# Two FNet and gated layers on one core: the second layer's downs of blocks two to four in seven products over six tile pairs

## The chip, the cores and the metric

The kernel runs on one core of a Trainium2 chip. TensorE (PE, with PEld for its weight loads), VectorE (DVE), ScalarE (ACT), GpSimd (POOL) and SyncE (SP, which here only issues DMAs) each run their own list of instructions in order and meet through semaphores. The metric is the device time of one execution in microseconds (us).

## The reference

The input x has 2048 rows of 640 numbers; the function is two equal layers, each an FNet mixing and a gated unit of width 1728 (the three weights are drawn eight times as large as the sizes 0.05 suggest).

```python
def _A_ref(x, dft_seq_re, dft_seq_im, dft_hid_re, dft_hid_im):
    a = jnp.einsum("bsd,ed->bse", x, dft_hid_re)
    b = jnp.einsum("bsd,ed->bse", x, dft_hid_im)
    return jnp.einsum("ts,bse->bte", dft_seq_re, a) - jnp.einsum("ts,bse->bte", dft_seq_im, b)

def _B_ref(x, w_gate, w_up, w_down):
    g = jnp.einsum("bsd,df->bsf", x, w_gate)
    u = jnp.einsum("bsd,df->bsf", x, w_up)
    return jnp.einsum("bsf,fd->bsd", _sigmoid(g) * u, w_down)

x = A_x
for _ in range(2):
    x = x + _A_ref(_layernorm(x, axis=-1), ...)
    x = x + _B_ref(_layernorm(x, axis=-1), B_w_gate, B_w_up, B_w_down)
return x
```

## The kernel before

**Numbers.** A float32 number is held as a high and a low float16 part; a product is three passes (high by high, high by low, low by high) summed in PSUM in float32. ACT makes a high part by a copy, DVE the low part by a subtraction.

**Tiles.** The 2048 rows are four blocks (NB) of 512 rows, a block four tiles (TB) of 128 rows. The gated width of 1728 is 13 full tiles of 128 (NF) and a tail of 64, tile 13. In layer 2, blocks two to four are b = 1, 2, 3 in the code.

**Gate and up of a block** (`seven`, from L1517). For each of the 13 tiles j, the products of the tile's gate and up weights with the block's turned rows are made by seven products of combined operands instead of eight; two tiles share one step. The rows, combined and turned (features on partitions), stand in `XW[place(b)]`, and two such places alternate. The gate's and up's results come out as 128x512 numbers `hv`; `up_parts` (L1508) splits them into a high and a low part (`ht`, L1513 on ACT and L1514 on DVE).

**Down of a block** (`down`, from L1593). For each of its four row tiles the 41 products (13 tiles by three passes, two for the tail) run into two PSUM banks, one for each half of the 640 columns: 328 matmuls of 128x320 in a block, and two adds onto x for each row tile (L1618). In layer 2 each finished row tile is then stored to the output (`store_x`, L442 and L447).

**Next block's rows.** While block b-1 is in its downs, the rows of block b are made in two pairs of row tiles, i = 0 and 1: `pair_stats`, `pair_scale`, `pair_apply` (L603), `pair_combine` (L610 to L613), `pair_parts` (L621, L622, four pieces) and `pair_transpose` (L628), which issues two DMA transposes on SP, one for the high and one for the low parts. PE needs all four before the first product of block b.

**Weights.** They are split once in layer 1 and kept in DRAM (`kept_w`, `kept_s`). `load_s` (L1362) brings the gate, combined and up weights of tile j back: three loads on SP (L1363, L1365, and L1367 or L1369).

**Structure tests.** The program tests that the DFT matrices have the structure that it uses. In layer 2, `load_hidden_rows` (L1724) loads rows of the hidden matrix from POOL's DMA queue, and DVE compares them (L1728, and L1687 to L1690 for the sequence matrix); `test_all` (L1761 on) gathers the results.

**What sets the order.** All work around the products is put at a time on a line of steps, `at(u, function, ...)`, where u counts steps from the start of the program and `block[b]` is the first of block b: a block has 14 for gate and up (one for each tile) and eight for its downs. Whatever falls to a step is written into the program there, and each engine runs what it gets in that order. Homes in SBUF are given by `Slots` and `find_homes`, which run once ahead without homes to learn who lives when; the areas for turned rows and for the down weights stand outside of them, in front of FIX.

The lines that set the rows' and first loads' times:

```python
u = block[b] - 8 + 1.2 * i
...
    at(u + 0.2 + 0.2 * n, pair_parts, b, i, n)
at(u + 1.1, pair_transpose, b, i, not first and b == last)
...
at(u - 2 - 0.5 * (j % 2) if j > 3 else block[b] - ((5.9, 3, 2, 1.5) if first and b == 1 else (8, 7.9, 4.5, 3.5))[j], load_s, j, not first and b == last)
```

## Time and profile before

| | |
|---|---|
| time, median of 3 runs | 1135.06 us (1134.55 to 1135.15) |
| span of the profiled execution | 1133.3 us |
| the profiled execution's own time | not listed apart; the median is 1.8 us above its span, taken as what lies around it |
| PE busy | 1117.1 us (99%) |
| DVE, ACT, POOL busy | 67%, 48%, 31% |
| four downs of layer 2 | 44.72 us each |
| gate and up of layer 2's third block | 79.7 us |

A group's row gives line, engine, operation, what it writes from what it reads, and the shape; then the count, the busy time, the mean duration, and the idle time of its engine just before with what ended it. In a timeline a row is a run of equal instructions with its start, its length and its count. A window's row gives the busy time of each engine in a stretch. Several rows are in the prediction.

### The profile page before, as it was taken

The page shows a single profiled execution, that of the slowest core. Times are in us where ns is not written, and L with a number is a line of the kernel's source. Part 1 is how long each engine was busy: PE and PEld are TensorE (multiplying, and loading weights), DVE is VectorE, ACT ScalarE, POOL GpSimd, SP SyncE. Part 2 cuts the span into 40 slices and gives each one's busy share as a digit, 9 for nine tenths or more (in the row PEclk, how much of TensorE's full clock was granted, in tenths as well). Part 3 has the DMA queues.
Part 4 walks back from the last instruction along what each step waited for, and adds up shares of the span by engine and source line. Part 5 has one row for each costly group of instructions (what it writes and reads, how often), then busy time and mean ns, then how long its engine had stood idle before and what let it go on. Part 6 is the DMA issues. An engine that isn't in the chain of part 4 may idle for free. (4 is left out here: it accounts for less than half of the span.)

```text
span 1133.3 us, 23690 instructions
## 1 busy us (share of the span) xinstructions
PE 1117.1 (99%) x9112; PEld 891.3 (79%) x9112; DVE 757.7 (67%) x1679; ACT 539.9 (48%) x1191; POOL 346.8 (31%) x568
## 2 busy tenths in 40 slices
PE   7999999999999999999999999999999999999997
PEld 5767446788878887788878888778877888788875
DVE  7984897856756776576667877834764678526751
ACT  7985583355525653256525545314542555225430
POOL 1001653343455354322340203031554222132001
PEclk9999999999999999999999999999999999999999
DMA  7633885878597756778521772585857873998411
GB/s 241 194 107 103 311 314 154 247 221 256 156 223 225 256 183 159 205 240 309 165 94 53 195 228 83 136 234 179 257 172 171 280 256 103 115 247 261 167 42 39
DMA packets 154448, 214.74 MB, mean 189 GB/s; under 512 B 74655, under 2 KB 99505, under 8 KB 154326
## 3 DMA queue, kind: packets, MB, share of 16 engines
q1 hardware_dynamic: 135622, 165.04, 50.0%
q0 software_dynamic: 18560, 47.93, 14.4%
q8 instruction: 73, 1.20, 0.4%
q14 instruction: 49, 0.40, 0.1%
q10 hardware_dynamic: 144, 0.16, 0.0%
HBM read 173.04 MB, written 25.44 MB: 175 GB/s over the span
## 5 line engine op out<-in xcount | busy, mean ns | idle before, releaser
L1446 PE MATMUL acc<-big 128*128 128x256 f16 x4698 | 516.4, 273 | 0.0
L1446 PEld LDWEIGHTS <-big 128*128 128x128 f16 x4698 | 459.7, 98 | 54.3
L1603 PE MATMUL acc<-big 128*128 128x320 f16 x2624 | 357.7, 299 | 0.0
L1603 PEld LDWEIGHTS <-big 128*128 128x128 f16 x2624 | 256.8, 98 | 99.5
L1450 ACT ACTIVATE big<-acc 128x256 f32<-128x256 f32 x348 | 131.1, 382 | 261.8 <-PE acc L1446 259.4
L1664 POOL DMA_DIRECT2D big<-in_ct x256 | 174.3, 686 | 249.5 <-DVE big L1673 110.3
L1514 DVE TENSOR_TENSOR big<-big 128x512 f16<-128x512 f32 x87 | 59.9, 688 | 111.6 <-ACT big L1513 111.5
L1636 ACT ACTIVATE big<-big 128x768 f32<-128x768 f32 (+10 forms) x110 | 81.3, 739 | 83.9 <-DVE big L1673 56.6
L1399 PE MATMUL acc<-big 128*128 128x256 f16 (+1 forms) x705 | 114.7, 325 | 0.3 <-ACT big L678 0.3
L1399 PEld LDWEIGHTS <-big 128*128 128x128 f16 x705 | 68.9, 98 | 44.9 <-issue 0.6
L1618 DVE SCALAR_TENSOR_TENSOR big<-acc,big 128x320 f32<-128x320 f32 x64 | 28.4, 483 | 74.3 <-PE acc L1603 74.3
L1492 ACT ACTIVATE big<-big 128x512 f32<-128x512 f32 x87 | 53.2, 627 | 44.5 <-DVE big L1483 43.8
L271 DVE SCALAR_TENSOR_TENSOR big<-big 128x640 f16<-128x640 f32 (+7 forms) x82 | 61.4, 779 | 11.1 <-ACT big L269 8.8
L1502 DVE SCALAR_TENSOR_TENSOR big<-acc,big 128x256 f32<-128x256 f32 x87 | 36.4, 418 | 48.2 <-PE acc L1446 42.7
L269 ACT ACTIVATE big<-big 128x640 f16<-128x640 f32 (+7 forms) x82 | 51.3, 658 | 21.0 <-POOL big L1337 6.6
L1483 DVE TENSOR_TENSOR big<-big,acc 128x512 f32<-128x512 f32 x87 | 59.2, 680 | 2.9 <-PE acc L1446 2.6
L1513 ACT ACTIVATE big<-big 128x512 f16<-128x512 f32 x87 | 54.4, 625 | 7.6 <-DVE big L1504 6.5
L1681 POOL DMA_DIRECT2D big<-in_ct x40 | 27.3, 688 | 92.2 <-ACT big L1636 55.9
L621 ACT ACTIVATE big<-big 128x384 f16<-128x384 f32 (+2 forms) x48 | 28.6, 646 | 52.3 <-DVE big L603 34.5
L442 POOL DMA_INDIRECT out<-big,rows x8 | 9.5, 1187 | 133.4 <-DVE fin L1761 53.6
L1482 DVE TENSOR_TENSOR big<-big 128x256 f32<-128x256 f32 x87 | 36.3, 417 | 8.8 <-ACT big L1450 8.7
L622 DVE TENSOR_TENSOR big<-big 128x384 f16<-128x384 f32 (+2 forms) x48 | 34.2, 750 | 7.1 <-DMA big<-big 7.0
(252 smaller groups left out, 1089.2 us busy)
## 6 DMA issues: line engine op xcount, KB each, us to landing
big<-kept_s SPq DMA_DIRECT2D x84, 512.0 KB, 7.1
big<-kept_w SPq DMA_DIRECT2D x115, 320.0 KB, 4.8
big<-in_ct POOLq DMA_DIRECT2D x256, 128.0 KB, 5.1
big<-kept_w SPq DMA_DIRECT2D x74, 192.0 KB, 5.8
kept_w<-big SPq DMA_DIRECT2D x27, 320.0 KB, 3.7
big<-in_ct POOLq DMA_DIRECT2D x32, 256.0 KB, 5.9
kept_s<-big SPq DMA_DIRECT2D x13, 512.0 KB, 7.6
big<-in_wg SPq DMA_DIRECT2D x18, 320.0 KB, 4.9
```

Of the source, the lines that this page charges most:

```text
L269: nc.scalar.activation(dh, src, AF.Copy, scale=s)
L271: nc.vector.scalar_tensor_tensor(dl, src, s, dh, op0=OP.mult, op1=OP.subtract)
L1399: nc.tensor.matmul(ps, w[wp][:, d * P : (d + 1) * P], xt[:, xp, :], start=(d == 0 and wp == HI and xp == HI), stop=(d == ND - 1 and wp == LO))
L1446: nc.tensor.matmul(ps, wt, xt, start=start and n == 0, stop=n == len(todo) - 1, skip_group_check=not start)
L1450: nc.scalar.activation(dst, ps, AF.Copy)
L1483: nc.vector.tensor_tensor(v, v, other, op=OP.add)
L1492: nc.scalar.activation(v, v, AF.Sigmoid, scale=SG)
L1513: nc.scalar.activation(s.parts[HI], v, AF.Copy)
L1514: nc.vector.tensor_tensor(s.parts[LO], v, s.parts[HI], op=OP.subtract)
L1603: nc.tensor.matmul(held["pd", e][0][:, :EH], held["ht", j].parts[hp][:, i * P : (i + 1) * P], held["w", 2, j].parts[wp][:, e * EH : (e + 1 ...
L1636: nc.scalar.activation(v, v, AF.Square, accum_out=new_sum()[:p])
L1664: nc.gpsimd.dma_start(v[:, g], bass.AP(ct.tensor, (r * S + row) * S, [[P, NS], [d * S, 16], [1, P]]))
```

## The change

In layer 2, for blocks two to four (`MADE`), the down runs over six pairs of tiles (0 to 11) with seven products of half the rows by half the columns each, instead of eight. A pair's left operand is the 2x2 of tile (two) by row half (two), its right one that of tile by column half; S1 to S4 are sums of left quarters, T1 to T4 of weights' quarters. The chains stay in PSUM: after an add onto x has read a bank, the next product goes on in it, so that one chain serves several quarters. Tiles 12 and 13 go by plain products. A block has 252 + 40 = 292 matmuls of the same shape, in eight steps, and 16 adds.

The left sums are made in layer 2 (`mates_sums`, four DVE operations of 128x256 for a pair) and split in four pieces (`mates_parts`: 512, 256, 512 and 512 columns, in place of 512 twice); the last pair's sums are split inside the down. The weights' sums are made in layer 1, in its second and third block: twelve loads of 320 KB, four POOL subtractions for each pair, a split on ACT and DVE, six stores of 640 KB. Layer 2 loads them back (`load_t`).

They lie there in the second place for turned rows: `place(b)` gives one place for all later blocks of layer 2. For blocks that follow a changed down, the pair work and the first loads get later times. `find_homes` learns of holes and pins, so that freed fixed areas can be used. WMAX, the largest weight that the program takes on this path, becomes 4.

```diff
-WMAX = 16.0
+WMAX = 4.0
...
+NP = 6
+MADE = {(1, 1), (1, 2), (1, 3)}
...
     def place(b):
-        return (b + len(other)) % 2
+        return 0 if other and b else (b + len(other)) % 2
...
+    def make_mates(m):
+        a, b = (held["tr", j].f32 for j in (2 * m, 2 * m + 1))
+        v = fixed(made_at(m) + 10, 10, "tf", m).f32
+        t1, t2, t3, t4 = (v[:, EH * n : EH * (n + 1)] for n in range(4))
+        nc.gpsimd.tensor_tensor(t1, a[:, EH:], a[:, :EH], op=OP.subtract)
+        nc.gpsimd.tensor_tensor(t3, b[:, EH:], a[:, EH:], op=OP.subtract)
+        nc.gpsimd.tensor_tensor(t2, b[:, EH:], t1, op=OP.subtract)
+        nc.gpsimd.tensor_tensor(t4, b[:, :EH], t2, op=OP.subtract)
...
+    def load_t(m):
+        pin = (0, 10, XU + XTU, XU + XTU + 10, XU + XTU + 20, FIX)[m]
+        nc.sync.dma_start(take(10, "T", m, pin=pin).f16, kept["t", m])
...
+        if ("hv", j) not in held:
+            if j % 2:
+                mates_parts(j - 1, "hA")
+                mates.append(j - 1)
+            return
...
+    def mates_sums():
...
+        a21, a11, a12, a22 = (v[:, 256 * n : 256 * (n + 1)] for n in range(4))
+        s1, s2, s3, s4 = (s[:, 256 * n : 256 * (n + 1)] for n in range(4))
+        nc.vector.tensor_tensor(s1, a21, a22, op=OP.add)
+        nc.vector.tensor_tensor(s3, a11, a21, op=OP.subtract)
+        nc.vector.tensor_tensor(s2, s1, a11, op=OP.subtract)
+        nc.vector.tensor_tensor(s4, a12, s2, op=OP.subtract)
+
+    PIECES = {"hA": ("hp", 256, 512), "hB": ("hp", 768, 256), "hS": ("hs", 0, 512), "hR": ("hs", 512, 512)}
+
+    def mates_parts(j, name):
+        key, o, n = PIECES[name]
+        src = held[key, j].f32[:, o : o + n]
+        h, l = take(n // 128, name, j, high=True).parts
+        nc.scalar.activation(h, src, AF.Copy)
+        nc.vector.tensor_tensor(l, src, h, op=OP.subtract)
...
+    A11, A12, A22, S1, S2, S3, S4 = range(7)
...
+    def mated_down(b, store):
...
+        for p in range(2):
+            todo += products_of(p, "a", A11, 0, True, True) + [(add, p, "a", p, 0, False)]
+        for p in range(2):
+            todo += products_of(p, "c", A12, 1, True, False)
+        todo += [(done, "hA")]
+        for p in range(2):
+            todo += products_of(p, "a", S2, 4, False, True) + [(add, p, "a", p, 1, False)]
+        for p in range(2):
+            todo += plain(p, "c", p, 0, False) + [(add, p, "c", p, 0, True)]
+        for p in range(2):
+            todo += products_of(p, "d", S1, 3, True, True) + [(add, p, "d", p + 2, 1, False)]
+        todo += [(done, "hS")]
+        for p in range(2):
+            todo += products_of(p, "a", S3, 5, False, True) + [(add, p, "a", p + 2, 1, False)]
+        for p in range(2):
+            todo += products_of(p, "d", S4, 2, False, False) + plain(p, "d", p, 1, False)
+            todo += [(add, p, "d", p, 1, True), (put, p)]
...
+                    if n == 38:
+                        mates_rest()
+                    if (n - cuts[k]) % 6 == 0 and n > 38:
+                        due((n - cuts[k]) / (cuts[k + 1] - cuts[k]))
...
-                u = block[b] - 8 + 1.2 * i
+                slow = (layer, b - 1) in MADE
+                u = block[b] - 6.9 + 1.8 * i if slow else block[b] - 8 + 1.2 * i
...
-                    at(u + 0.2 + 0.2 * n, pair_parts, b, i, n)
-                at(u + 1.1, pair_transpose, b, i, not first and b == last)
+                    at(u + (0.4 + 0.3 * n if slow else 0.2 + 0.2 * n), pair_parts, b, i, n)
+                at(u + (1.5 if slow else 1.1), pair_transpose, b, i, not first and b == last)
...
-                        at(u - 2 - 0.5 * (j % 2) if j > 3 else block[b] - ((5.9, 3, 2, 1.5) if first and b == 1 else (8, 7.9, 4.5, 3.5))[j], load_s, j, not first and b == last)
+                        at(u - 2 - 0.5 * (j % 2) if j > 3 else block[b] - ((5.9, 3, 2, 1.5) if first and b == 1 else (4.5, 4, 3, 2.2) if (layer, b - 1) in MADE else (8, 7.9, 4.5, 3.5))[j], load_s, j, not first and b == last)
```

Three places in the program show what moves. First DVE, where the third block of layer 2 goes over from its gate and up into its downs, up to the first work on the fourth block's rows. Before, L1687 to L1690 are a test of the sequence matrix, L1482 to L1504 the last tile's up, L1514 its low part, L603 the rows:

```order
L1687 TENSOR_REDUCE cmax<-big 1x1
L1688 TENSOR_TENSOR big<-big 1x256
L1689 TENSOR_TENSOR big<-big 1x256
L1690 TENSOR_TENSOR big<-big 1x256
L1482 TENSOR_TENSOR big<-big 128x256
L1483 TENSOR_TENSOR big<-big,acc_481 128x512
L1502 SCALAR_TENSOR_TENSOR big<-acc_480,big 128x256
L1504 SCALAR_TENSOR_TENSOR big<-big 128x256
L1514 TENSOR_TENSOR big<-big 128x512
L603 TENSOR_SCALAR big<-big,small_84 128x640 x2
```

The same place after the change; L1574 and L1576 are L1502 and L1504, L1591 is the low part of a tile pair's first piece, L1782 the adds of a changed down, L1916 to L1919 the test, L1615 the low parts of the last pair's other pieces, and L633 the rows:

```order
L1574 SCALAR_TENSOR_TENSOR big<-acc_479,big 128x256
L1576 SCALAR_TENSOR_TENSOR big<-big 128x256
L1591 TENSOR_TENSOR big<-big 128x512
L1782 SCALAR_TENSOR_TENSOR big<-acc_481,big 128x320
L1782 SCALAR_TENSOR_TENSOR big<-acc_64,big 128x320
L1916 TENSOR_REDUCE cmax<-big 1x1
L1917 TENSOR_TENSOR big<-big 1x256
L1918 TENSOR_TENSOR big<-big 1x256
L1919 TENSOR_TENSOR big<-big 1x256
L1615 TENSOR_TENSOR big<-big 128x512 x2
L1615 TENSOR_TENSOR big<-big 128x256
L633 TENSOR_SCALAR big<-big,small_84 128x640 x2
```

Two adds and three low parts now stand ahead of the rows, and so does a test (its second) that stood behind the rows' parts before.

Second SP, in the downs of the third block, with the fourth block's rows (L628, after the change L658) and first weights:

```order
L1363 DMA big<-kept_w_0_1146 128x1280
L1365 DMA big<-kept_s_2103 128x2048
L1367 DMA big<-kept_w_0_1163 128x1280
L1363 DMA big<-kept_w_1_1182 128x1280
L1365 DMA big<-kept_s_2204 128x2048
L1367 DMA big<-kept_w_1_1199 128x1280
L628 DMA_TRANSPOSE big<-big 128x17x128 x2
L447 DMA out<-big 128x640
L628 DMA_TRANSPOSE big<-big 128x17x128 x2
L1363 DMA big<-kept_w_2_1253 128x1280
```

After the change (L1347 is another weight's load):

```order
L1347 DMA big<-kept_w_0_1906 128x1280
L658 DMA_TRANSPOSE big<-big 128x17x128 x2
L1426 DMA big<-kept_w_0_1146 128x1280
L1428 DMA big<-kept_s_2103 128x2048
L1430 DMA big<-kept_w_0_1163 128x1280
L1426 DMA big<-kept_w_1_1182 128x1280
L1428 DMA big<-kept_s_2204 128x2048
L1430 DMA big<-kept_w_1_1199 128x1280
L658 DMA_TRANSPOSE big<-big 128x17x128 x2
L1426 DMA big<-kept_w_2_1253 128x1280
```

The six loads of tiles 0 and 1 stood ahead of both pairs of transposes and now stand between them; the store moved away from there.

Third POOL, in the same downs: loads of the hidden matrix's rows (L1724, after the change L1953), of the sequence matrix's (L1681 and L1910), and the stores of finished rows (L442 and L472).

```order
L1681 DMA big<-in_ct 1x2x256 x2
L1724 DMA big<-in_wh 100x4x128 x4
L442 DMA out<-big,rows 2048x640
L1724 DMA big<-in_wh 100x4x128 x2
L442 DMA out<-big,rows 2048x640
L1724 DMA big<-in_wh 100x4x128 x10
```

After the change:

```order
L508 TENSOR_SCALAR small_77<-small_77 128x2
L1910 DMA big<-in_ct 1x2x256 x2
L1953 DMA big<-in_wh 100x4x128 x6
L472 DMA out<-big,rows 2048x640 x2
L1953 DMA big<-in_wh 100x4x128 x10
```

Two loads (one test's rows) now stand ahead of a store behind which they stood.

More of the change, by code (lines that the diff above doesn't have):

```diff
@@ L1549, in mm @@
                 gate(i)
+            if not last:
+                mates_rest()
             some(0)
@@ L1873, in folded @@
             d0 = len(steps)
-            for i in range(TB):
+            for i in range(TB) if (layer, b) not in MADE else ():
                 if b == NB - 1 and i == TB - 1:
@@ L1879, in folded @@
                     steps.append(down(b, i, j0, j1, not first))
+            if (layer, b) in MADE:
+                steps += mated_down(b, not first)
         end = len(steps)
@@ L2062, in some, with due @@
                     f(*a)
-        if two:
+        def due(part):
+            while todo and todo[0][0] - u <= part:
+                _, f, a = todo.pop(0)
+                f(*a)
+        if spans_two:
             mm(some)
+        elif two:
+            mm(due)
         else:
```

228 lines of the change are left out of this document (189 added, 39 removed).

## The prediction

> **What bounds the kernel now.** I read the page's first and fourth parts, then its groups.
>
> ```profile
> span 1133.3 us, 23690 instructions
> PE 1117.1 (99%) x9112; PEld 891.3 (79%) x9112; DVE 757.7 (67%) x1679; ACT 539.9 (48%) x1191; POOL 346.8 (31%) x568
> PE 44%; issue 1%; ACT 0%; POOL 0%; DVE 0%
> L1603 PE MATMUL acc<-big 128*128 128x320 f16 x2624 | 357.7, 299 | 0.0
> L1618 DVE SCALAR_TENSOR_TENSOR big<-acc,big 128x320 f32<-128x320 f32 x64 | 28.4, 483 | 74.3 <-PE acc L1603 74.3
> ```
>
> PE is busy for 99% of the span, and the chain of work that ended last holds almost nothing else. The matmuls of the downs (L1603) never waited; the adds behind them (L1618) waited for PE. PE's list of waits begins with the kernel's opening, and its rows come to some 10 us in all, none at a down or behind one:
>
> ```profile
> PE twin L404 <- DMA big<-in_x: 6.1, 3, 3.9
> ```
>
> So a matmul taken out of a down is time off the end, as long as PE still finds its next operand ready. PE's timeline gives the price of one, and the table by stage shows what surrounds it (one block's down, the gate and up of the next block, that block's down):
>
> ```profile
> 958.28 44.72 PE L1603 MATMUL acc<-big 128*128 128x320 f16 x328
> 833.82:878.54 44.72, 44.72 (x332) 32.25 (x330) 24.11 (x57) 12.50 (x24) 17.25 (x24) 1.00 0.71 173
> 878.54:958.28 79.74, 79.74 (x733) 71.46 (x732) 57.66 (x134) 43.04 (x99) 22.30 (x42) 1.00 0.67 218
> 958.28:1003.00 44.72, 44.72 (x331) 32.19 (x329) 21.18 (x44) 11.14 (x22) 9.24 (x8) 1.00 0.97 137
> ```
>
> The columns behind the stretch are its length and the busy us (with count) of PE, its weight loads, DVE, ACT and POOL, then granted clock, DMA share and GB/s. A down of 328 matmuls takes 44.72 us, 136.3 ns each at clock 1.00. Below, T is the start of a down.
>
> **The matmuls.** Seven products over six tile pairs, two row halves and three passes are 252 matmuls of the same shape; tiles 12 and 13 keep 40. That is 292 instead of 328, so a changed down lasts 292 x 0.1363 = 39.8 us. Three blocks lose 36 each: 108 x 0.1363 = **14.7 us off**.
>
> **The operands of the downs.** Each pair of tiles needs four more sums (128x256) and its halves split in pieces of 512, 512, 512 and 256 instead of two of 512. The rows for such operations:
>
> ```profile
> L1514 DVE TENSOR_TENSOR big<-big 128x512 f16<-128x512 f32 x87 | 59.9, 688 | 111.6 <-ACT big L1513 111.5
> L1482 DVE TENSOR_TENSOR big<-big 128x256 f32<-128x256 f32 x87 | 36.3, 417 | 8.8 <-ACT big L1450 8.7
> ```
>
> Per pair DVE gains 4 x 0.417 + 0.688 + 0.417 = 2.8 us and a block 17 us, nearly all in the gate and up, where DVE is busy for 57.7 of 79.7 us: about 72 of 79.7 after. It fits, and I cost it at nothing there; if a step did not fit, its excess would be paid in each of six steps. The last pair's pieces are made in the down itself. PE wants that pair's first low part at its 18th matmul, T+2.3; the chain of S2 goes on in the first banks from the 73rd, T+9.8, when the adds must have read them, and wants its last low part near the 89th, T+12.1. By DVE's order and these durations the three are ready at T+1.6, T+9.8 and T+12.1. Sixteen adds instead of eight cost DVE 3.9 us more per down, beside PE; by the same count the later adds have 1.4 to 2.5 us to spare. Bounds: 0 to 1 us at each of the two tight places in three downs; I take **+0.5 us** altogether.
>
> **The turned rows.** This decides. The next block's rows are normalized and combined on DVE, then go through two pairs of DMA transposes on SP (L628). With one place for turned rows and later due times, they start later, and the six loads of the next gate's first two tiles now stand on SP between the pairs, where one store stood. DVE's and SP's timelines in the downs that start at 833.82 and 958.28, then the answer on L628:
>
> ```profile
> 841.03 1.13 DVE L603 TENSOR_SCALAR big<-big,small 128x640 f32<-128x640 f32 x2
> 965.73 1.13 DVE L603 TENSOR_SCALAR big<-big,small 128x640 f32<-128x640 f32 x2
> 845.34 6.18 SPq L628 DMA_TRANSPOSE big<-big  x2
> ...
> 859.78 6.43 SPq L628 DMA_TRANSPOSE big<-big  x2
> 866.26 1.13 SPq L1363 DMA_DIRECT2D big<-kept_w  x1
> ...
> 869.72 0.53 SPq L1369 DMA_DIRECT2D big<-kept_w  x1
> 970.04 12.39 SPq L628 DMA_TRANSPOSE big<-big  x2
> 982.53 1.49 SPq L447 DMA_DIRECT2D out<-big  x1
> 984.12 13.74 SPq L628 DMA_TRANSPOSE big<-big  x2
> 997.92 0.59 SPq L1363 DMA_DIRECT2D big<-kept_w  x1
> ...
> 1001.94 0.74 SPq L1367 DMA_DIRECT2D big<-kept_w  x1
> L628 SPq DMA_TRANSPOSE big<-big x24: 2247/3132/10562, 190.0 to 994.7; - x24
> DMA to landing us min/median/max: 8.3/9.4/11.1
> ```
>
> Before, DVE reaches the first pair's rows at T+7.2 or T+7.5, and the transposes follow 4.3 us later. The last transpose was issued at 994.7; with the least landing time of 8.3 us it landed at 1003.0, and the next gate starts at 1003.00. So before the third of these boundaries has **no slack**, and the second about 6 us (859.78 + 3.2 + 9.4 = 872.4 against 878.54).
>
> After, DVE does ahead of those rows: four sums, two adds, three low parts and, in the third block's down, four rows of a structure test that stood behind. By the starts in DVE's list (0.34 us apart for 256 wide, 0.6 for 512, 0.45 for an add) that is 1.4 + 0.9 + 1.5 + 1.6 = 5.4 us, and about 0.5 of waiting for ACT's high parts: rows at T+13.1 and transposes at T+16.9 (second block's down) and T+17.8 (third's). Now the sums.
>
> Second block's down: a pair of transposes holds SP 6.2 us, six loads 4.0 (866.26 to 870.25), so the second pair could go at T+27.1; DVE has it at T+27.7. It lands 3.2 + 9.4 = 12.6 us later, T+40.3 against the down's end at T+39.8. But the loads ahead carry 2 x (320 + 512 + 192) KB = 2.1 MB, which at the rate of a stretch full of such loads, 317 GB/s, takes 6.6 us of all DMA engines; if the transposes stand behind all of it, T+44. Bounds 0 to 4.5; I take the middle, **+2.5 us**.
>
> Third block's down: here transposes run beside small loads of the hidden DFT matrix that POOL issues (L1724). The windows, POOL's rows, and the landing of L1724's loads up to here:
>
> ```profile
> 847.00:851.00 4.00, 4.00 (x32) 2.90 (x30) 0.62 (x1) 0.00 (x0) 0.00 (x0) 1.00 1.17 229
> 878.54:894.00 15.46, 15.46 (x144) 13.85 (x143) 8.84 (x21) 6.72 (x18) 6.29 (x10) 1.00 1.05 317
> 972.00:994.00 22.00, 22.00 (x164) 15.85 (x162) 9.03 (x19) 3.84 (x8) 2.31 (x2) 1.00 1.30 106
> 969.58 2.42 POOL L1724 DMA_DIRECT2D big<-in_wh  x2 [14.98 <-ACT big L1636]
> 976.32 2.31 POOL L1724 DMA_DIRECT2D big<-in_wh  x2 [4.33 <-ACT big L1636]
> 996.76 2.38 POOL L1724 DMA_DIRECT2D big<-in_wh  x2
> DMA to landing us min/median/max: 8.4/11.2/16.5
> ```
>
> Transposes alone move 229 GB/s (847 to 851); beside two of these loads 106 GB/s, with the DMA engines fuller (1.30), and a pair takes 12.39 or 13.74 us instead of 6.2. After, the second load's release on ACT moves with the pair's parts to about T+17, beside the first pair, and the third, moved ahead of a store on POOL, to about T+28, near the second pair. So I let both pairs stay slow: 17.8 + 12.4 + 4.8 (six loads, 997.92 to 1002.68) + 13.7 = T+48.7 for SP's end, and landing 5.2 us later as before (997.86 to 1003.0), T+53.9. The gate could start at T+39.8: a wait of **+14.0 us**. Its ends: 1.5 if no transpose is slowed (17.8 + 6.2 + 4.8 + 12.6 = T+41.4), 17 if a load lands late inside the second pair. I take the value built from this stage's own rows.
>
> [...]
>
> **The clock behind such a wait.** The stretch after the last matmul (1127.6), and PE's first two groups of one form:
>
> ```profile
> 1130.00:1131.00 1.00, 0.00 (x0) 0.00 (x0) 0.00 (x0) 0.00 (x0) 0.00 (x0) 1.00 0.02 8
> 1132.00:1133.30 1.30, 0.00 (x0) 0.00 (x0) 0.00 (x0) 0.00 (x0) 0.00 (x0) 0.50 0.04 13
> 3.88 4.78 PE L404 MATMUL twin<-big 128*128 128x320 f32 x8 [3.88 <-DMA big<-in_x]
> 11.76 2.39 PE L404 MATMUL twin<-big 128*128 128x320 f32 x8 [1.64 <-DMA big<-in_x]
> ```
>
> The granted clock falls to 0.50 about 4 us after PE stops, and the eight matmuls that open the kernel take 4.78 us, the same eight later 2.39. A wait longer than 4 us so costs 0 to 2.4 us more at half speed; nearest is the opening, and I take **+2.0 us** once, at the third boundary. [...]
>
> **What lies beside other work.** Layer 1 makes the weights' combinations: 24 POOL subtractions, six splits on ACT and DVE, 7.9 MB of traffic. The nearest POOL row is 1.17 us for 256 columns:
>
> ```profile
> L1337 POOL TENSOR_TENSOR big<-big 128x256 f32<-128x256 f32 x13 | 15.2, 1166 | 64.8 <-DVE big L271 38.7 <-DVE big L622 12.2 <-ACT big L1589 6.3
> 310.31 16.00 SPq L628 DMA_TRANSPOSE big<-big  x4
> 434.78 20.32 SPq L628 DMA_TRANSPOSE big<-big  x4
> ```
>
> At 320 columns some 1.5 us, 35 us of an engine that is busy 31%; the transposes of layer 1 (the two rows of four) have no wait of PE behind them. Nothing there, or layer 2's six loads of 640 KB, which have a whole block's time: 0, and at most 1 us if the cover is gone.
>
> **Sum**, against the profiled execution's own time: 1133.3 of span and 1.8 around it, if that execution stands where the median of the three runs does (1135.06; the lowest is 0.5 below): -14.7 + 0.5 + 2.5 + 14.0 + 2.0 = +4.3, **1139.3 us**. A measurement here can tell 0.2%, 2.3 us, from no change: 1132.8 to 1137.3 counts as the same.
>
> **Rivals.** A is the forecast; its own range, 1134 to 1143, is that of the two waits. *B, one pair slow*: for it speaks that the third hidden load may miss the transposes. 17.8 + 12.4 + 4.8 + 12.6 = T+47.6, a wait of 7.8 in place of 14.0: 1133.1. *C, in time*: no transpose is slowed, the loads drain at once; waits of 0.5 and 1.5, no fall of the clock: 1135.1 - 14.7 + 0.5 + 2.0 = 1122.9. For it speaks the pace of the second block's down; against it, that the slow pairs before had the same company. [...] *D, both boundaries late*: the second block's transposes run at layer 1's pace (16.0 to 20.3 us for four, up to 10.2 a pair) because the loads stand among them: 16.9 + 10.2 + 4.0 + 10.2 + 5.2 = T+46.5, a wait of 6.7 and a second fall of the clock: 1139.3 + 4.2 + 2.0 = 1145.5. Waits and clock together decide: above 14.2 us it is slower than before. *E, the saving isn't there*: chains wait for their adds by about 2 us for each of seven products, 14 in three downs: 1135. Against it stand the spare times above.
>
> **Chances.** A 0.42, B 0.20, C 0.24, D 0.09, E 0.05. Slower by over 0.2%: 0.30 of A and D, 0.39. Faster: C, half of B and 0.01 of A, 0.35. The same: the rest, 0.26. The range runs from C's lower part to the upper part of A with D's beginning, 1122 to 1144; outside lie a part of C and most of D.
>
> **What would show it.** Right: the changed downs hold 292 matmuls; PE waits for a transpose (DMA big<-big) at the start of the fourth block's gate, 10 us or more, with the granted clock below 1.00 behind it, and for 1 to 4 us at the third's; SP's rows show transposes, six loads, transposes, and 12 us for a pair beside L1724's loads. Wrong: no PE wait at these starts (C), pairs of 6 us in the third block's down (C or B), or downs of over 41 us with PE waiting for DVE's adds (E).

## The result and the profile after

The changed kernel takes 1152.82 us (median of 4 runs, 1147.59 to 1153.55) where the kernel before took 1134.98: a ratio of 1.0145, 95% interval 1.0125 to 1.0166. It is slower, by four times what was forecast (1139.3), and outside the range. The profiled execution took 1153.06 us with a span of 1151.3.

The page's first and fourth parts:

```profile
span 1151.3 us, 23739 instructions
PE 1111.2 (97%) x9004; PEld 882.6 (77%) x9004; DVE 828.8 (72%) x1817; ACT 557.0 (48%) x1233; POOL 370.9 (32%) x592
PE 31%; DVE 6%; DMA 5%; issue 2%; ACT 1%; SPq 1%; POOL 0%; DVEq 0%; ACTq 0%; POOLq 0%
```

DMA and DVE are now on the chain that ended last, which before held almost PE alone. PE's list of waits (us in total, times, longest), without the rows of the opening that it had before too:

```profile
PE acc L1509 <- DMA big<-big: 7.3, 4, 3.0
PE acc L1509 <- DMA big<-kept_w: 6.0, 3, 3.9
...
PE acc L1509 <- ACT big L1513: 3.8, 4, 1.9
PE acc L1717 <- ACT big L1590: 3.3, 2, 2.5
...
PE acc L1762 <- DVE big L1782: 0.9, 1, 0.9
```

L1509 are the gate's and up's products (L1446 before), L1717 the plain downs, L1762 the new ones; DMA big<-big are the transposes, kept_w the weights' loads, L1513 and L1590 are ACT's copies of a product and of a high part.

The start of layer 2's first down, which is not changed, in PE's timeline of before and of after:

```profile
709.35 44.72 PE L1603 MATMUL acc<-big 128*128 128x320 f16 x328
```

```profile
716.83 44.72 PE L1717 MATMUL acc<-big 128*128 128x320 f16 x328
```

The table by stage of after, which answers to the one in the prediction:

```profile
841.29:881.30 40.01, 39.96 (x294) 28.56 (x292) 31.82 (x75) 15.15 (x29) 12.57 (x19) 1.00 0.73 163
881.30:968.70 87.40, 80.56 (x733) 71.50 (x732) 66.51 (x159) 43.03 (x105) 29.77 (x50) 1.00 0.68 224
968.70:1009.70 41.00, 40.12 (x294) 28.48 (x292) 29.57 (x63) 14.42 (x29) 7.04 (x6) 1.00 0.64 118
1009.70:1103.84 94.14, 84.63 (x733) 73.64 (x732) 58.89 (x121) 40.46 (x105) 13.99 (x14) 0.95 0.71 207
1103.84:1151.30 47.46, 39.83 (x294) 28.47 (x291) 22.18 (x59) 8.91 (x27) 2.95 (x4) 0.97 0.08 31
```

| from, to | before | after | difference |
|---|---|---|---|
| start to layer 2's first down | 709.35 | 716.83 | +7.5 |
| first down, second block's gate and up | 124.47 | 124.46 | 0.0 |
| second block's down | 44.72 | 40.01 | -4.7 |
| third gate and up, with its first wait | 79.74 | 87.40 | +7.7 |
| third block's down | 44.72 | 41.00 | -3.7 |
| fourth gate and up, with its first wait | 79.86 | 94.14 | +14.3 |
| fourth down and the end | 50.44 | 47.46 | -3.0 |

So the downs give what was worked out (39.8 us and a wait of 0.9 in one), and 31 us are lost around them: 7.5 in layer 1, 7.7 and 14.3 in the two gates and 1.9 at the end.

SP's timeline around the third and fourth gates' starts (881.6 and 1012.7):

```profile
858.11 5.22 SPq L658 DMA_TRANSPOSE big<-big  x2
...
867.17 14.29 SPq L658 DMA_TRANSPOSE big<-big  x2
...
883.32 0.54 SPq L477 DMA_DIRECT2D out<-big  x1
...
897.90 0.26 SPq L479 DMA_DIRECT2D out<-big  x1
...
987.04 9.39 SPq L658 DMA_TRANSPOSE big<-big  x2
996.54 1.29 SPq L1426 DMA_DIRECT2D big<-kept_w  x1
...
1000.53 12.55 SPq L658 DMA_TRANSPOSE big<-big  x2
1013.18 0.73 SPq L1426 DMA_DIRECT2D big<-kept_w  x1
```

POOL's and DVE's timelines behind the third gate's start, then SP's list of waits there:

```profile
890.64 1.08 POOL L472 DMA_INDIRECT out<-big,rows  x1 [20.24 <-DMA out<-big]
```

```profile
895.32 0.42 DVE L1899 TENSOR_TENSOR big<-big 128x256 f32<-128x256 f32 x1 [11.75 <-DMA big<-in_ct]
```

```profile
SPq L479 <- DMA out<-big,rows: 12.3, 1, 12.3
```

The second pair, behind the six loads, takes 14.29 us where the first takes 5.22. And a second thing is seen: the stores. A down's first row tile is now complete only when S4 is, some 29 us into the down; its store (L477) stands on SP behind the transposes and three more loads, and goes at 883.32 (859.35 before). POOL's store (L472) waits for it to land, 20.24 us; the sequence test's loads (in_ct) stand behind that on POOL, so DVE waits 11.75 us for them with the gate's adds queued behind; and SP's last stores (L479) wait for POOL's, 12.3 us, with the gate's weight loads behind them. Of the 4.9 us that PE waits inside the third gate, 1.7 are for such a load (kept_w) and 3.2 for ACT. ACT squares the test's differences (L1865) between its copies of products (L1513), and so waits for DVE's test, as ACT's and PE's timelines show:

```profile
897.67 0.84 ACT L1865 ACTIVATE big<-big 128x768 f32<-128x768 f32 x1 [5.80 <-DVE big L1902]
```

```profile
898.92 3.76 PE L1509 MATMUL acc<-big 128*128 128x256 f16 x33 [1.25 <-ACT big L1513]
```

### The profile page after: what moved, and what is told of

Its sections match the earlier page's. It is cut to its first block, busy times and chain, and to the rows that moved or that the text cites. A ratio compares the mean times of both kernels' runs of the same rounds, so it can differ in the third digit from the quotient of the medians.

```text
span 1151.3 us, 23739 instructions
## 1 busy us (share of the span) xinstructions
PE 1111.2 (97%) x9004; PEld 882.6 (77%) x9004; DVE 828.8 (72%) x1817; ACT 557.0 (48%) x1233; POOL 370.9 (32%) x592
## 5 line engine op out<-in xcount | busy, mean ns | idle before, releaser
L1509 PE MATMUL acc<-big 128*128 128x256 f16 x4698 | 522.2, 274 | 17.2 <-DMA big<-big 7.3
L1509 PEld LDWEIGHTS <-big 128*128 128x128 f16 x4698 | 461.4, 98 | 75.8 <-issue 12.8
L1513 ACT ACTIVATE big<-acc 128x256 f32<-128x256 f32 x348 | 128.3, 381 | 239.0 <-PE acc L1509 229.4
L1717 PE MATMUL acc<-big 128*128 128x320 f16 x1640 | 226.0, 301 | 3.4 <-ACT big L1590 3.3
L1717 PEld LDWEIGHTS <-big 128*128 128x128 f16 x1640 | 160.8, 98 | 67.7 <-ACT big L1590 4.0
L1865 ACT ACTIVATE big<-big 128x768 f32<-128x768 f32 (+10 forms) x110 | 81.4, 740 | 83.3 <-DVE big L1902 59.0
L1762 PE MATMUL acc<-big 128*128 128x320 f16 x756 | 105.6, 300 | 0.9 <-DVE big L1782 0.9
L1462 PEld LDWEIGHTS <-big 128*128 128x128 f16 x705 | 68.9, 98 | 44.9 <-issue 0.6
L1762 PEld LDWEIGHTS <-big 128*128 128x128 f16 x756 | 73.9, 98 | 30.0 <-issue 1.2
L301 DVE SCALAR_TENSOR_TENSOR big<-big 128x640 f16<-128x640 f32 (+8 forms) x88 | 70.6, 832 | 17.9 <-ACT big L299 15.5
L1591 DVE TENSOR_TENSOR big<-big 128x512 f16<-128x512 f32 x51 | 36.4, 713 | 56.7 <-ACT big L1590 56.7
L299 ACT ACTIVATE big<-big 128x640 f16<-128x640 f32 (+8 forms) x88 | 59.0, 700 | 23.0 <-POOL big L1367 8.0
L1615 DVE TENSOR_TENSOR big<-big 128x512 f16<-128x512 f32 x72 | 41.5, 620 | 27.2 <-ACT big L1614 27.2
L1910 POOL DMA_DIRECT2D big<-in_ct x40 | 27.3, 687 | 86.5 <-ACT big L1865 30.2
L1552 DVE TENSOR_TENSOR big<-big 128x256 f32<-128x256 f32 x87 | 38.1, 438 | 22.6 <-ACT big L1513 22.5
L1574 DVE SCALAR_TENSOR_TENSOR big<-acc,big 128x256 f32<-128x256 f32 x87 | 36.4, 418 | 22.9 <-PE acc L1509 19.1
L1900 DVE TENSOR_TENSOR big<-big 128x256 f32<-128x256 f32 x64 | 30.1, 471 | 25.6 <-DMA big<-in_ct 25.6
```

The source lines that it names most:

```text
L299: nc.scalar.activation(dh, src, AF.Copy, scale=s)
L301: nc.vector.scalar_tensor_tensor(dl, src, s, dh, op0=OP.mult, op1=OP.subtract)
L1462: nc.tensor.matmul(ps, w[wp][:, d * P : (d + 1) * P], xt[:, xp, :], start=(d == 0 and wp == HI and xp == HI), stop=(d == ND - 1 and wp == LO))
L1509: nc.tensor.matmul(ps, wt, xt, start=start and n == 0, stop=n == len(todo) - 1, skip_group_check=not start)
L1513: nc.scalar.activation(dst, ps, AF.Copy)
L1615: nc.vector.tensor_tensor(l, src, h, op=OP.subtract)
```

## The experiments

Times beside the kernel before, run on the same chip each time (its medians lay between 1134.98 and 1135.71). All start from the changed kernel.

**Layer 1's work.** e5 leaves it out, with the loads of layer 2 kept (two of 320 KB for one of 640).

```diff
-        for m in range(NP):
+        for m in range(NP) if not first else ():
...
-        nc.sync.dma_start(take(10, "T", m, pin=pin).f16, kept["t", m])
+            nc.sync.dma_start(t[:, 1280 * k : 1280 * k + 1280], kept["w", 0, 2 * m + k])
```

> Leaves out layer 1's making of the weights' sums (loads, POOL subtractions, splits, stores); layer 2 loads the same number of bytes of gate weights in their place, so the products of S1 to S4 use other numbers. If layer 1's work costs what the shift of layer 2's first down says (7.5 us later than before), that shift falls below 1 us and the kernel comes to about 1146. If the shift is only a scatter of the opening or of the clock, 3 us or more of it stay and the time is above 1150.

1147.54 us, 5.3 below. PE's timeline: layer 2's first down starts where it did before the change (709.35).

```profile
709.43 44.72 PE L1719 MATMUL acc<-big 128*128 128x320 f16 x328
```

So all 7.5 us of the shift are that work's; the time falls by 2 less. The shift is not the same in each execution: in the profiles of the nine versions whose layer 1 has this work unmoved (the changed kernel, e2 to e4, e7, e12 and e15 to e17), layer 2's first down starts 2.3 (e12) to 10.2 us (e3) later than before. Which part of the work it is, three moves were to tell. e1 starts it earlier (some of its products then have other numbers), e6 puts the three pairs of a block closer, e9 moves only the third pair's split and store behind the last tile's up:

```diff
-                u = block[1 + m // 3] + 6.5 + 2.6 * (m % 3)
+                u = block[1 + m // 3] + 4.5 + 2.2 * (m % 3)
```

> The layer 1 work on the weights' sums begins 2 steps earlier in its blocks and lies 2.2 instead of 2.6 steps apart, so the third pair's split no longer stands on DVE between the tail tile and the last tile's up. Theory K (that split, and POOL's subtractions beside DVE, delay the last tile's chain on DVE): PE's waits for L1590 at the starts of layer 1's second and third block's downs (0.85 and 2.5 us, with 1.9 us at half clock behind) go, and the kernel gains 4 to 6 us, about 1148. Rival T (the 7.8 MB of extra transfers delay the weights' loads): those waits stay or move to loads of kept_w, gain below 1 us.

```diff
-                u = block[1 + m // 3] + 6.5 + 2.6 * (m % 3)
+                u = block[1 + m // 3] + 6.5 + 1.8 * (m % 3)
```

> The three pairs of a block in layer 1 lie 1.8 steps apart instead of 2.6, the first where it was. Theory K (the third pair's split on ACT and DVE, and POOL's subtractions beside DVE, stand ahead of the last tile's up): PE's waits for L1590 at the second and third block's downs (0.85 and 2.5 us) fall below 0.5 each and the half clock behind them goes; about 3 to 5 us faster, 1148 to 1150. Rival Q (SP's stores of the sums hold the weights' loads behind them until the split is done): new waits for kept_w inside the gates eat it up, gain below 1.5 us.

```diff
-                at(u + 2, split_mates, m, (0,))
+                at(u + (3 if late_one else 2), split_mates, m, (0,))
```

> In layer 1 only the third pair's split (one step of ACT, one of DVE) and its store move from ahead of the last tile's up to behind it, into the down, ahead of the second pair of rows. Theory K: PE's waits for L1590 at the second and third block's downs (0.85 and 2.5 us with 1.9 of half clock) go, layer 1's shift falls from 7.5 to about 2.5, and the kernel gains 3 to 5 us: 1148 to 1150. Rival P (POOL's subtractions beside DVE and the added transfers make the delay): the waits stay above 1 us together, gain below 1.5 us.

All three are slower than the changed kernel: 1157.91, 1157.64 and 1156.72 us, with layer 2's first down 10.9, 15.0 and 11.9 us later than before in their profiles. e9's list of waits in layer 1 (300 to 500 us) fits theory K, without the gain:

```profile
PE acc L1509 <- DMA big<-big: 8.2, 2, 4.5
```

The waits for L1590 are gone, as K says; in their place the next gates wait 8.2 us for transposes. The split and SP's store of the sums now stand ahead of the second pair of rows, but that this is the reason is not shown: e3, whose layer 1 is not moved, has one such wait of 4.1 us too. By their lists, e6 keeps a wait for L1590 of 3.1 us and adds 6.5 us of waits inside the gates, e1 has none for L1590 and 6.7 inside. Each of the places tried costs something. In the changed kernel's layer 1 one more thing is seen: beside POOL's subtractions, DVE takes 1.05 us for a subtraction of the size that takes 0.42 at 895.32 above (DVE's timeline, then POOL's):

```profile
428.44 1.05 DVE L1900 TENSOR_TENSOR big<-big 128x256 f32<-128x256 f32 x1
```

```profile
428.18 1.03 POOL L1405 TENSOR_TENSOR big<-big 128x320 f32<-128x320 f32 x1
```

**Stores.** e2 issues the first row tile's store of blocks two to four on ACT's queue.

```diff
-            on = nc.scalar if (i, g, c.stop) == (NB - 1, GD, D) else nc.sync
+            on = nc.scalar if (i, g, c.stop) == (NB - 1, GD, D) or (i and g == GA) else nc.sync
```

> The first row tile's store of layer 2's later blocks is issued on ACT's queue instead of SP's, where it stood behind the transposes and two tiles' loads. Theory S (the stores wait for each other through the output tensor, and POOL's and SP's loads stand behind the waiting stores): POOL's first indirect store goes at about 33 us behind the start of the down instead of 49 (890.6), DVE's wait of 11.75 us for in_ct falls below 4, PE's waits inside the two gates (4.9 us in the third block, 3.95 and 2.6 of slow clock in the fourth) fall below 2 us together, and the kernel gains 6 to 11 us, about 1144. Rival L (PE's late start after the transposes shifts ACT's and DVE's order): the waits inside the gates stay within 1 us each, time the same.

1146.00 us, 6.8 below, where theory S had it. The span of its profile is 7.7 us below; 3.5 of these lie in layer 1, which the edit does not touch, and 4.1 in layer 2, all in the fourth gate (table at the end of this section). And it was not by the theory's whole path: POOL's store goes at 880.85, 43 us into the down and not 33, and DVE still waits 10.97 us for in_ct (POOL's timeline of e2, then DVE's):

```profile
880.85 1.09 POOL L472 DMA_INDIRECT out<-big,rows  x1 [13.91 <-DVE wmax L292]
```

```profile
891.51 0.43 DVE L1899 TENSOR_TENSOR big<-big 128x256 f32<-128x256 f32 x1 [10.97 <-DMA big<-in_ct]
```

The waits inside the gates fall from 4.9 to 2.2 us and from 3.95 to none, while the waits for transposes rise (2.0 to 3.9 and 5.3 to 7.1). In the fourth gate, PE's wait of 3.95 us for kept_w in the changed kernel comes behind a store on SP that waits for POOL's (SP's list of waits there):

```profile
SPq L477 <- DMA out<-big,rows: 12.0, 1, 12.0
```

In e2 this wait of SP is 1.7 us and PE's is gone, so there the chain of stores holds SP's weight loads. In the third gate the wait for kept_w stays (1.7 us, 2.2 in e2), and what goes is PE's wait for ACT: DVE's part of the test is done 14 us behind the gate's first waits in the changed kernel and 12 in e2, and ACT's wait for it falls from 5.80 to 2.00 us (ACT's timeline of e2):

```profile
893.96 0.85 ACT L1865 ACTIVATE big<-big 128x768 f32<-128x768 f32 x1 [2.00 <-DVE big L1902]
```

**Loads between the pairs.** e3 puts the six loads behind both.

```diff
-(4.5, 4, 3, 2.2) if (layer, b - 1) in MADE
+(3.5, 3.4, 3, 2.2) if (layer, b - 1) in MADE
```

> The six loads of tiles 0 and 1 stand behind both pairs of transposes instead of between them. If the loads' data slow the second pair (14.1 us on SP in the second block's down, 12.5 in the third's), it takes 6 to 7 us in the second block's down, PE's waits for transposes (2.0 and 5.3 us) go, and a wait for kept_w of 0 to 3 us may come at the gates' starts: 2 to 6 us faster. If the second pair is slow of itself, it stays above 10 us, and the gates wait for loads too: the same or slower.

1148.18 us, 4.6 below. SP's timeline of e3: in the second block's down the second pair takes 7.00 us instead of 14.29, and the third gate starts without a wait; in the third block's down, beside the hidden rows' loads, the four still take 19.84:

```profile
868.79 7.00 SPq L658 DMA_TRANSPOSE big<-big  x2
...
988.46 19.84 SPq L658 DMA_TRANSPOSE big<-big  x4
```

There the gate then waits for kept_w instead (3.3 us, and 4.6 later on), and the third gate waits 4.8 us for ACT. The six loads ahead do slow a pair, by 7.3 us (14.29 to 7.00); that e3 is faster for it is not shown. Its times (1146.55 to 1154.83) overlap with the changed kernel's, and in its profile, of its slowest execution, layer 2 takes as long up to the last matmul as in the changed kernel's.

**Hidden rows' loads.** e4 starts them 7.5 steps later, e7 6.5 steps later with e2's store, e8 also with e3 and e6.

```diff
-(r, k), 15.5 + 1.95 * (4 * r + k), 3.2)
+(r, k), 23 + 1.95 * (4 * r + k), 3.2)
```

> The loads of the hidden matrix's rows begin 7.5 steps later, behind the third block's down. If they slow the transposes beside them, the first pair of that down takes 5 to 6.5 us on SP instead of 9.3 and the second 12.5 less 0 to 3, and the fourth block's first wait (5.3 us) falls by 3 to 5; the wait for kept_w inside that gate stays, since the chain of stores stays: 3 to 6 us faster. If the slow pair has another cause, it stays at 9 us or more and the time within 1 us.

> The first row tile's store on ACT's queue (as in e2_store_act) and the hidden rows' loads 6.5 steps later, behind the third block's down. Store theory and contention theory together: the fourth block's first waits (3.98 and 3.13 us in e2_store_act) fall below 2 together, since its pairs take 5 and 8 to 9 us on SP, and the half clock behind goes: 6 to 8 us below e2_store_act's 1146, 1138 to 1141. If the loads between the pairs alone make that wait, it stays above 5 us and the time above 1144.

> e7_store_and_hidden with the six loads behind both pairs and the sums of layer 1 closer together. If the four costs add up: no wait above 1 us for transposes at the two boundaries; layer 1's shift 7.5 down to 4; the tail and the adds stay (1.9 and 0.9): about 1130, the first time below the kernel before. If the loads behind the pairs come late instead, waits for kept_w of 3 to 5 us at each boundary: about 1138.

These three took 4221, 4218 and 4221 us. The tests' rooms in SBUF are freed in the order of loading; with the new times a test read a room that was already given away, and the program ran its general path behind the fast one. Only their rows up to there can be read. They tell the disputed cost by itself: the third block's pairs in SP's timeline of e4, without hidden rows' loads beside them and with the six loads still between:

```profile
988.83 5.06 SPq L658 DMA_TRANSPOSE big<-big  x2
...
998.07 8.46 SPq L658 DMA_TRANSPOSE big<-big  x2
```

9.39 and 12.55 fall to 5.06 and 8.46, and the fourth gate starts at once in all three. With the stores left as they were, the wait for kept_w inside that gate falls too, from 3.95 to 0.67 us (e4's PE), against what was expected:

```profile
1034.41 49.30 PE L1509 MATMUL acc<-big 128*128 128x256 f16 x450 [0.67 <-DMA big<-kept_w]
```

The whole gate takes 80.6 us instead of 94.1: 13.6 of the 14.3 us lost there go with these loads alone. In e8, with the loads behind the pairs too, neither gate waits for transposes. e10 and e11 then moved the loads closer together so that the tests keep their order (22 + 1.15 instead of 15.5 + 1.95), with e9's split and e2's store, e11 with e3's order as well:

> e9_late_split, the first row tile's store on ACT's queue, and the hidden rows' loads behind the third block's down, closer together than in e7 (so that the tests keep their order). If the costs add: layer 1 2 to 3 us, third block's start and gate 4 to 5, fourth block none, adds 1, tail 1, against 14.7 saved: 1128 to 1131. If moving the hidden rows' loads only moves the contention to the fourth gate's weights: waits for kept_w of 3 us or more there, about 1136.

> e10_three_moves with the six loads behind both pairs of transposes. The second block's second pair takes 6 us on SP instead of 14 and the third gate's first wait (4 us) goes; the wait for ACT inside that gate (3.5 us, DVE behind the sequence tests, behind POOL's stores) comes instead. If these are one for one, the time is that of e10 within 1.5 us; if the transposes' wait is worth more, 2 to 4 us below it.

1152.22 and 1144.25 us. The closer loads collide with the weights of the fourth gate, which lasts 90.3 us in e10 and 89.0 in e11, with waits for kept_w of 8.4 and 7.3 us in all; with e9's split, layer 2's first down is 9.8 and 10.6 us late. Here the rival held.

**Together.** e12 frees the rooms by name, so that the hidden rows' loads can keep their spacing behind the down, with e2's store, e3's order, and layer 1 as it was. e13 leaves layer 1's work out as well.

```diff
-                k = n_room.pop(0)
+                k = done - 1
...
-(r, k), 15.5 + 1.95 * (4 * r + k), 3.2)
+(r, k), 22 + 1.95 * (4 * r + k), 3.2)
```

> Store on ACT's queue, six loads behind both pairs, hidden rows' loads 6.5 steps later at their old spacing, with the tests' rooms freed by name so that their order may change; layer 1 as in the changed kernel. If the three costs add: no wait for transposes above 1 us at layer 2's boundaries, one wait of some 3.5 us in the third gate, the fourth gate at 81 to 83 us; layer 1 as it falls (2.4 to 7.5): 1134 to 1140. If another wait takes their place: above 1144, as e11_four_moves.

> e12_three_moves that leaves out layer 1's making of the weights' sums (layer 2 loads gate weights in their place). If layer 1's work costs the 5.3 us that e5 showed, on top: 1129 to 1134, below the kernel before. If the costs don't add (layer 1's lateness is taken up later anyway): the time of e12 within 2 us.

e12: 1134.83 us (12 runs, 1130.75 to 1141.36), 18 below the changed kernel, 1.0006 of before with an interval of 0.9992 to 1.0021. Its list of waits from 150 us on has no transpose and no kept_w left:

```profile
PE acc L1509 <- ACT big L1513: 4.0, 2, 3.1
PE acc L1717 <- ACT big L1590: 1.7, 1, 1.7
PE acc L1762 <- DVE big L1782: 0.6, 1, 0.6
PE acc L1762 <- DVE big L1615: 0.4, 1, 0.4
```

The time is what was expected if the three costs add. By the stages they nearly do: from layer 2's first down to the last matmul, e12 is 15.7 us shorter than the changed kernel, where e2, e3 and e4 are 4.1, 0.1 and 10.5 shorter. e12's profile, though, is of an execution of 1131.44 us, one of its fast ones. e13: 1134.40 us, within 2 us of e12: leaving layer 1's work out gains nothing here, against what e5 said. In its profiled execution layer 2's first down starts only 1.9 us sooner than in e12's, and the end after the last matmul takes 9.4 us instead of 6.8, with the same stores.

**The last block alone** (`MADE = {(1, 3)}`), without layer 1's work and with it:

> Only the last block's down is changed, with no block behind it and layer 1's work left out (gate weights loaded in place of the sums). Boundary theory (what was lost in layer 2 was lost where rows, loads and stores crowd ahead of the next block): 4.9 us saved less about 1 for an add and 1 to 2 at the tail: 1131 to 1133. Rival G (the gates' extra DVE and ACT work and the downs' own waits cost it): 1135 or more, with waits inside the last gate or down.

> Only the last block's down is changed, with layer 1's work as in the changed kernel. By e5 (5.3 us for layer 1's work) 5 us above e14_last_down_no_layer1, 1136 to 1138, slower than before; if layer 1's lateness is caught up by slack in layer 2, within 2 us of e14.

1134.31 and 1137.52 us. In e14 the last matmul ends at 1122.6, 5.0 us sooner than before, and nothing waits; but the span ends only 0.8 us sooner, since the end after it takes 9.9 us instead of 5.7. SP's list of waits at the end of e14:

```profile
SPq L477 <- DMA out<-big,rows: 12.5, 1, 12.5
SPq L234 <- SPq L234: 3.0, 1, 3.0
```

The last row tile's first half waits on SP for POOL's stores of the tiles before, up to 1125.3, and then SP's branch takes 3.0 us to its next instruction. Boundary theory holds for layer 2's gates, and the end was priced too low. With layer 1's work (e15) it is 3.2 us slower than without, slower than before (1.0025, 1.0015 to 1.0035); layer 2's first down starts 3.8 us later.

**The end.** e16 is e12 with the last row tile stored by one DMA on ACT's queue; e17 has the six loads ahead of both pairs too (5.6 and 5.5 steps ahead of the block).

```diff
-                todo += [(put, 3, slice(0, EH))] if last else [(put, 3)]
+                todo += [(put, 3)]
```

> e12_three_moves, and the last row tile is stored by one DMA on ACT's queue at the end instead of two halves on SP's and ACT's. If SP's flag load, branch and the 3 us to its next instruction stand on the path behind its half, the time from the last matmul's end to the span's end falls from 6.8 (7.6 in the changed kernel) to 5 to 6 us: 1 to 2 us below e12, 1133 to 1134. If ACT's own branch sets the end, within 0.5 us of e12.

> e16_one_last_store with the six loads ahead of both pairs of transposes, the order of the kernel before. If their room in SBUF is free by then, both pairs take 5 to 7 us on SP, the loads have landed long before the gate, and it is within 1 us of e16 or up to 3 us faster. If a load waits for its room, SP holds the first pair behind it, and the boundaries wait 2 to 6 us each: slower than e16 by 4 to 10 us.

e16: 1134.39 us (1.0 us below its runs of before; ratio 0.9992, 0.9978 to 1.0007), the end 6.0 us (1126.85 to 1132.8) instead of 6.8: the mechanism as expected, the gain within the scatter. e17: 1136.53, neither of its cases: both gates start at once, but PE waits inside the second block's down (its list there, then DVE's timeline):

```profile
PE acc L1762 <- DVE big L1782: 3.4, 1, 3.4
```

```profile
869.14 1.29 DVE L652 TENSOR_TENSOR big<-big 128x384 f16<-128x384 f32 x2 [5.25 <-DMA big<-big]
870.36 0.48 DVE L1782 SCALAR_TENSOR_TENSOR big<-acc,big 128x320 f32<-128x320 f32 x1
```

The first pair's transposes, behind the loads, keep the second pair's parts from their room, and an add stands behind those on DVE.

**By stage.** Since layer 1's shift differs from execution to execution, layer 2 is better compared from its own first down. By PE's timelines (us; a gate counts from the end of the down ahead of it, with its first waits; e4's end is that of the general path and left out):

| version | layer 2's first down starts | third gate | fourth gate | first down to the end of the last matmul | end behind it |
|---|---|---|---|---|---|
| before | 709.35 | 79.7 | 79.9 | 418.2 | 5.7 |
| changed | 716.83 | 87.4 | 94.1 | 426.8 | 7.6 |
| e2, store | 713.35 | 88.0 | 89.5 | 422.7 | 7.5 |
| e3, loads behind | 719.53 | 86.4 | 95.3 | 426.7 | 6.6 |
| e4, hidden rows later | 716.43 | 89.6 | 80.6 | 416.3 | |
| e12, all three | 711.69 | 84.7 | 80.8 | 411.1 | 6.8 |
| e13, e12 without layer 1's work | 709.78 | 85.1 | 80.8 | 412.0 | 9.4 |
| e16, e12 with one last store | 714.58 | 85.8 | 80.8 | 412.3 | 6.0 |
| e17, e16 with loads ahead | 716.88 | 79.8 | 80.8 | 411.4 | 5.6 |

The five versions whose layer 2 has the changed kernel's order (it, e1, e5, e6, e9) lie between 424.2 and 430.1 us in the column before the last. So the hidden rows' loads are clear of this spread; the store's 4.1 us are just outside it, and e3's 0.1 is inside. With all three moved, layer 2 keeps about half of the 14.7 us that the matmuls save, and layer 1's work takes 2.3 to 7.5 of them in e12, e16 and e17. No version tried beats the kernel before by what can be measured.

## Why the prediction was wrong, step by step

- **The matmuls, -14.7.** Right: PE was busy for 40.0, 40.1 and 39.8 us in the three downs.
- **The operands of the downs, +0.5.** Right in size: one wait of 0.9 us for an add (L1762 <- L1782), at the place named.
- **Second block's boundary, +2.5.** Right: 2.0 us (881.64 and 883.54, waits of 0.4 and 1.6).
- **Third block's boundary, +14.0.** The mechanism was right, the size of the wait was not: 5.3 us. The chain was worked out as 17.8 + 12.4 + 4.8 + 13.7 + 5.2; measured, from 968.70, 18.3 + 9.4 + 4.0 + 12.6 + 2.2. The largest errors are the first pair, which was slowed less, and the last term, 3 us each: I took the landing from the view's 8.3 us and concluded that before had no slack, but here PE goes 4.5 us after the last transpose's issue (1010.77 to 1015.28). The contention was confirmed by e4, the part of the six loads by e3. That the whole stage lost 14.3 us, near the 14.0 and 2.0 of wait and clock in the sum, is luck in the number: what PE did not wait for transposes it lost at a low clock (0.95 over the stage) and inside the gate.
- **The clock, +2.0.** Measured more, at more places. Windows behind three waits (2.5 us at 440, 3.0 and 2.3 with one matmul between at 1015, 3.95 at 1043; granted clock in the third column from the end):

```profile
440.04:445.04 5.00, 4.99 (x24) 2.87 (x25) 4.93 (x10) 3.12 (x6) 1.61 (x3) 0.66 0.10 37
1015.28:1020.28 5.00, 5.00 (x33) 3.85 (x33) 0.00 (x0) 0.77 (x2) 0.00 (x0) 0.69 1.00 354
1043.46:1049.40 5.94, 5.94 (x30) 4.31 (x31) 2.47 (x6) 2.76 (x6) 0.00 (x0) 0.53 1.04 243
```

  Against equal numbers of matmuls at full clock (256, 80 and 450 of them, at 0.136 us each for the first, as in the unchanged downs, and 0.109 for the others, 71.39 us for 654 in the chain of before; a row ends 0.17 us later than the chain has it, 44.72 and 44.55 in a down), the rows of 36.81, 10.38 and 52.03 us cost 1.9, 1.5 and 2.7 us, 6.0 together. That a wait under 4 us costs nothing was wrong. Behind the wait of 2.5 us the granted clock stood at 0.50 from 442.00 to 444.00; behind that of 3.95 us it was 0.50 from the first matmul (1043.46) to 1048.50. Behind the 0.4 and 1.6 us at the third gate it stayed at 1.00.
- **Layer 1, 0 to 1.** This step failed first: 7.5 us in the profile, 5.3 by e5, and 2.3 to 10.2 in the profiles of versions with the same layer 1. I priced POOL's 35 us and the bytes, and not the last tile's chain on DVE behind the third split, nor the store of the sums on SP. In the changed kernel PE's waits for ACT (0.85, 0.40 and 2.50 us) and the low clock behind the last make 5.6 of the 7.5. That the work is the cause is shown by e5; by which way it delays PE is argued from the lists, since no move of it made the kernel faster.
- **Gate and up, 0.** This step failed too: 4.9 us of waits in the third and 3.95 in the fourth. DVE had the room that was worked out (72 of 79.7 us forecast, 66.5 busy in a longer stage). What stopped the third gate was the chain of stores, through SP's weight loads and through the test that DVE and ACT waited for; in the fourth, moving the store (e2) or the hidden rows' loads (e4) each takes the wait away (3.95 us to none, and to 0.67). I wrote that a store moved away from between the pairs, and did not follow who waits for it.
- **The end**, which the sum left out: +1.9 us in the changed kernel, as the second last and the last store wait in one chain (SP waits 10.3 us there for POOL's stores) and SP's branch comes behind (2.9 us). e16, which takes SP's half of the last store away, shortens it by 0.8 us against e12.

The table's differences come to +18.1 (18.0 by the spans). With 14.7 saved, 32.8 us were lost where the forecast had 19.0. The wait that was priced 8.7 us too high hid part of what was left out. Rival D was nearest in time by the wrong mechanism: the second block's boundary, which it made late, cost 2.0 us. C, no wait at the gates, did not come: in before, transposes moved 229 GB/s with little beside them (847 to 851, 0.15 of the 0.92 MB on POOL's queue), against 317 in the stretch of plain loads (878.54 to 894).

## What to carry to other kernels

When work moves, follow what each moved store and load stands ahead of on its queue, and who waits for that one's landing: here most of layer 2's loss went when small loads no longer ran beside the transposes (10.5 us by e4's stages), and some when a store was issued sooner (4.1 by e2's). Before a few us between two times are put down to an edit, compare the stages that the edit does not touch: here the start of layer 2 alone differed by up to 8 us between versions with the same layer 1. This kernel, at 99% PE, had little room in the last steps of each block, also in blocks far from the change (layer 1's work cost 5.3 us by e5): work put there must be placed among DVE's, SP's and the transposes' order, not summed against an engine's idle share. A saving in the last block counted only as far as the end of the program (stores in a chain, branch) could follow: in e14 the last matmul ended 5.0 us sooner and the span 0.8.

## What the runs showed of the hardware that was not expected

- A 128x256 subtraction on DVE took 1.05 us (428.44, changed kernel) while POOL ran 128x320 subtractions, instead of 0.42 (895.32). It is not always DVE that is slowed: there, from 303.05, a 128x512 low part on DVE took 0.68 us, as elsewhere (0.69 at 424.15), and POOL's subtraction beside it 1.40 instead of 0.87 (411.37).
- Half clock (0.50 from 442.00 to 444.00, changed kernel) followed a wait of PE of 2.5 us.
- A pair of transposes took 5.06 (e4) and 5.22 us (changed kernel) on SP with little beside it, 9.39 beside POOL's small loads, 8.46 behind six loads in the third block's down (e4) and 14.29 in the second's, 12.55 with both.
- The time scatters by version: 1134.49 to 1137.70 us before (22 runs beside e16 and e17), 1147.59 to 1153.55 after (4 runs), 1130.75 to 1141.36 in e12 (12 runs). Part of it is in layer 1, by the starts of layer 2's first down. What sets which of these an execution gets stays open, and so does why e13 gains nothing over e12.
